# Reordering the first layer norm, one input load and two groups of short matmuls in a two-branch kernel on one core

## The chip, the cores and the metric

The kernel runs on one core of a Trainium2 chip. The metric is the device time of one execution in microseconds (us). All times inside the kernel are counted from the start of the profiled span.

## The reference, cut to what matters

```python
def reference(A_x, A_wqkv, A_w_phi, A_wo, B_x, B_w1, B_w2, B_w3, B_w4):
    xn = layernorm(A_x)                       # A_x is (1, 2048, 448); all bf16
    return A_x + A(xn, A_wqkv, A_w_phi, A_wo) + B(xn, B_w1, B_w2, B_w3, B_w4)

def A(x, wqkv, w_phi, wo):                    # linear attention, 16 heads of 28
    q, k, v = heads(x @ wqkv)
    phi(t) = concat(softmax(t @ w_phi), softmax(-t @ w_phi))
    kv, z  = phi(k).T @ v, sum(phi(k))        # sums over the 2048 rows
    return merge((phi(q) @ kv) / (phi(q) @ z + 1e-6)) @ wo

def B(x, w1, w2, w3, w4):                     # MLP with shifted columns
    h  = gelu(layernorm(x) @ w1)              # w1, w2: 448 x 448
    x1 = x + shift_quarters(h) @ w2
    return x1 + gelu(layernorm(x1) @ w3) @ w4 # w3: 448 x 1792, w4: 1792 x 448
```

The layer norm is over the 448 columns of one row. B normalises its input again; the kernel uses the once normalised rows for the product with w1.

## The kernel before

**Tiles.** The 2048 rows are 16 tiles of 128 rows (tile 0 to 15) and 4 groups of 4 tiles. `xtok` holds x, `xn` the normalised rows, `xnT` their transposes, with the 448 columns on partitions in four chunks of 128 (kc 0 to 3). 448 is not a multiple of 128: the chunks start at columns 0, 128, 192 and 320, and chunks 1 and 2 overlap by 64 columns. So a product over the 448 columns is three matmuls over 128 rows ("fulls") and one over 64 rows ("tail").

**Quads.** `quad` (L454) computes four such products into four PSUM banks: first the twelve fulls, three for each bank, with small jobs ("fills") put behind each bank's three; then the four tails. A tail uses rows 0 to 63 for an even bank and rows 64 to 127 for an odd one, so two of them run at a time in the two halves of the array. `w1_quad(g, ...)` (L470) does group g's product with w1 (output 112 x 512 for each bank) and empties the banks, two at a time, with a GELU on ScalarE into `hT`. `v_quad(i, ...)` (L477) does V of tiles i to i+3 (128 x 448 each) and empties the banks with copies into `vaug`, on ScalarE for the first eight tiles.

**The first layer norm** (L417 to L425, called at L626 to L634). For each tile VectorE makes the statistics (`ln_stats`: bn_stats and bn_aggr), GpSimd turns the variance into a scale (`ln_scale`: an add and a power of -1/2, into `rs`), and VectorE, or GpSimd for tiles 8, 10, 12 and 14, applies mean and scale (`ln1_apply`, written `xn<-xtok`). The program order on VectorE is written out: for tiles 0 to 7, statistics of tile i and then the normalise of tile i-1. From tile 8 on it goes by pairs.

**Loads** (L337 to L351). x tiles 0 to 3 come one by one, from the queues of SyncE (SP) and ScalarE; `load_x(4, 4)`, `load_x(8, 4)` and `load_x(12, 4)` bring four tiles in one transfer of 448 KB each, from SyncE. The V columns of wqkv (`wv`) and `w1` come in two halves of 224 KB each; w1 from ScalarE's queue. Behind the x loads SyncE issues w2, wphi and eight transposing loads of Wqkv (`wT`, in the region `hi`).

**Order of work on TensorE** (L635 to L648). After some matmuls that only keep it busy (`spin`), TensorE transposes tiles 0 to 11 itself: `xn_T(i, b)` (L445) is four transposes into bank b and one copy by ScalarE into `xnT`. The transposes of tiles 2 and 3 are fills of the V quad of tile 0, those of 4 to 7 fills of the W1 quad of group 0, and so on:

```python
v_quad(0, (4, 5, 6, 7), ([(xn_T, 2, 2)], [(xn_T, 3, 3)]))
w1_quad(0, (0, 1, 2, 3), ([], [], [(xn_T, 4, 4), (xn_T, 5, 5)], [(xn_T, 6, 6), (xn_T, 7, 7)]))
v_quad(4, (4, 5, 6, 7), ([], [], [(xn_T, 8, 0)], [(xn_T, 9, 1)]))
w1_quad(1, (0, 1, 2, 3), ([], [(xn_T, 10, 4)], [(xn_T, 11, 5)], [(phi_blocks,)]))
for i in range(12, 16):
    xn_Td(i)
```

Tiles 12 to 15 are transposed by DMA from SyncE's queue (`xn_Td`, L451), which then loads w3, wo and w4. The W1 quads of groups 2 and 3 follow, with `fold` (L438) as fills: it multiplies wphi into the Q and K columns of Wqkv, through banks 0 and 1 in group 2's quad and banks 4 and 5 in group 3's. `phi_blocks` (L431) makes the block matrix `bd` for it, with a product on VectorE. Then come the K and Q quads, the w2 products, the attention and the MLP (L658 on), about 160 us that the change doesn't touch.

**Waits.** A recorder (L18 to L185) keeps the order of each engine as it is written, finds for each instruction what it must wait for, and emits the waits. An engine's instructions run in program order, so one that waits holds all behind it on that engine. Every operation has the line of a recorder's helper in the profile: L188 is a matmul, L192 a transpose on TensorE, L196 a ScalarE activation, L200 an operation of VectorE or GpSimd, L203 a transposing DMA, L206 a plain DMA.

Of the kernel before, what the change touches and what calls it, by code (L numbers as in the profile page):

```python
# [5 lines left out]
ACT = mybir.ActivationFunctionType  # L6
# [202 lines left out]
def bass_parallel_sum__linear_kernel_hedgehog__mixer_s_mlp__prompt_kernel(  # L209
    nc, A_x, A_wqkv, A_w_phi, A_wo, B_x, B_w1, B_w2, B_w3, B_w4, out,  # L210
):
    _, S, D = A_x.shape
    H, DH = A_w_phi.shape[0], A_w_phi.shape[1]
    F = B_w3.shape[1]
    assert (S, D, H, DH, F) == (2048, 448, 16, 28, 1792)
    NT, NG, KC, NC, NM, FC, HP = 16, 4, 4, 4, 4, 14, 32
    CR = 112
# [5 lines left out]
    with es:  # L223
        R = Recorder(nc, es)
# [9 lines left out]
        def view(h, cols, dt=BF16, at=0):  # L234
            a = h[:, at // 2:at // 2 + cols * DTB[dt] // 2]
            return a if dt == BF16 else a.bitcast(dt)

        def new(name, cols, dt=BF16):
            return view(region(name, cols * DTB[dt]), cols, dt)

        pairs = []
        for b in range(4):
            t = es.enter_context(nc.psum_tensor("bank%d%d" % (2 * b, 2 * b + 1), [128, 1024], F32))
            R.track(t, 4096, psum=True)
            pairs.append(t)
        banks = [pairs[b // 2][:, 512 * (b % 2):512 * (b % 2) + 512] for b in range(8)]
# [5 lines left out]
        xnT = view(xnT_r, KC * S).rearrange("p (c s) -> p c s", c=KC)  # L252
        hT_r = region("hT", NM * HW * 2)
        hT = view(hT_r, NM * HW).rearrange("p (m s) -> p m s", m=NM)
# [3 lines left out]
        vaug = view(vaug_r, NT * 512).rearrange("p (t c) -> p t c", t=NT)  # L258
        gT = new("gT", 2 * KC * 512).rearrange("p (b c s) -> p b c s", b=2, c=KC)
# [4 lines left out]
        wv = new("wv", KC * D).rearrange("p (c d) -> p c d", c=KC)  # L264
# [4 lines left out]
        w1 = view(w1_r, KC * D).rearrange("p (c d) -> p c d", c=KC)  # L269
        w2 = new("w2", NM * D).rearrange("p (m d) -> p m d", m=NM)  # L270
        wo = new("wo", KC * D).rearrange("p (c d) -> p c d", c=KC)
        w3 = new("w3", KC * F).rearrange("p (c f) -> p c f", c=KC)
# [50 lines left out]
        dve, pool = "DVE", "POOL"  # L323


        def load_x(i, n, eng="SP"):
            R.dma(xtok[:, i:i + n, :], x2d[128 * i:128 * (i + n), :].rearrange("(j p) d -> p j d", p=128), eng)
# [5 lines left out]
        def load_lap(dst, src, engs=("SP", "SP")):  # L333
            for h in range(2):
                R.dma(dst[:, 2 * h:2 * h + 2, :], src[192 * h:192 * h + 256, :].rearrange("(c p) d -> p c d", p=128), engs[h])
# [3 lines left out]
        load_x(2, 1)  # L339
        load_lap(wv, A_wqkv[:, 896:1344], ("ACT", "SP"))  # L340
        load_x(3, 1, "ACT")
        load_x(4, 4)
        load_lap(w1, B_w1, ("ACT", "ACT"))
        load_x(8, 4)
        load_x(12, 4)
# [53 lines left out]
        def halves(a):  # L399
            return a.rearrange("p (b e) -> p b e", b=2)  # L400
# [12 lines left out]
        def ln_apply(eng, dst, src, mvt, rst, i):  # L413
            m, op = (mvt[:, i, 0:1], ALU.subtract) if eng == dve else (rst[:, i, 1:2], ALU.add)
            R.ew(eng, "tensor_scalar", dst, src, m, rst[:, i, 0:1], op0=op, op1=ALU.mult)
# [6 lines left out]
        def ln1_apply(eng, i):  # L422
            ln_apply(eng, halves(xn[:, i, :]), lap(xtok[:, i, :]), mv, rs, i)
# [27 lines left out]
        def xn_Td(i):  # L451
            R.dma_t(xnT[:, :, 128 * i:128 * i + 128], xn[:, i, :])

        def quad(outs, lhs, rhs, fills=(), more=()):  # L454
            for k in range(4):
                for kc in (0, 3, 2 - k % 2):
                    R.mm(outs(k), lhs(k, kc, 0, 128), rhs(k, kc, 0, 128), kc == 0, False)
                if k < len(fills):
                    for f in fills[k]:
                        f[0](*f[1:])  # L460
            for k in range(4):
                kc, lo = 1 + k % 2, 64 * (k % 2)
                R.mm(outs(k), lhs(k, kc, lo, lo + 64), rhs(k, kc, lo, lo + 64), False, True)
            for f in more:
                f()

        def two(b):
            return pairs[b // 2].rearrange("p (b e) -> p b e", b=2)

        def w1_quad(g, bs, fills=()):  # L470
            quad(lambda k: banks[bs[k]][0:CR, :],
                 lambda m, kc, lo, hi: w1[lo:hi, kc, CR * m:CR * m + CR],
                 lambda m, kc, lo, hi: xnT[lo:hi, kc, 512 * g:512 * g + 512], fills)
            for m in (0, 2):
                R.act(hT[0:CR, m:m + 2, 2 + 512 * g:2 + 512 * g + 512], two(bs[m])[0:CR, :, :], ACT.Gelu_apprx_tanh)

        def v_quad(i, bs, fills=()):  # L477
            quad(lambda k: banks[bs[k]][:, 0:D],
                 lambda k, kc, lo, hi: xnT[lo:hi, kc, 128 * (i + k):128 * (i + k) + 128],
                 lambda k, kc, lo, hi: wv[lo:hi, kc, :], fills)  # L480
            for k in (0, 2):
                vd = vaug[:, i + k:i + k + 2, :].rearrange("p t (h e) -> p t h e", e=HP)[:, :, :, 0:DH]
                vs = two(bs[k])[:, :, 0:D].rearrange("p t (h e) -> p t h e", e=DH)
                if i < 8:
                    R.act(vd, vs, ACT.Copy)
                else:
                    R.ew(dve, "tensor_copy", vd, vs)

        def kq_quad(i, bs):
            g, c = divmod(i, 4)  # L490

            def outs(k):
                return banks[bs[k]][:, 0:D] if k < 2 else banks[bs[k]][0:CR, :]

            def lhs(k, kc, lo, hi):
                if k < 2:
                    return xnT[lo:hi, kc, 128 * (i + k):128 * (i + k) + 128]
                return wpq[lo:hi, kc, CR * (c + k - 2):CR * (c + k - 1)]

            def rhs(k, kc, lo, hi):  # L500
                return wpk[lo:hi, kc, :] if k < 2 else xnT[lo:hi, kc, 512 * g:512 * g + 512]

            quad(outs, lhs, rhs)
            for s in range(2):
                R.act(phik[:, i:i + 2, s, :], two(bs[0])[:, :, 0:D], ACT.Exp, scale=1.0 - 2.0 * s)
            e = (eq_lo if g < 2 else eq_hi)[0:CR, c:c + 2, :, 512 * (g % 2):512 * (g % 2) + 512]
            for s in range(2):
                R.act(e[:, :, s, :], two(bs[2])[0:CR, :, :], ACT.Exp, scale=1.0 - 2.0 * s)
# [79 lines left out]

        def w3_quad(q, more=()):
            gf = [divmod(4 * q + k, FC) for k in range(4)]  # L590
            quad(lambda k: banks[k][:, :],
                 lambda k, kc, lo, hi: w3[lo:hi, kc, 128 * gf[k][1]:128 * gf[k][1] + 128],
                 lambda k, kc, lo, hi: gT[lo:hi, gf[k][0] % 2, kc, :], (), more)
            for k in (0, 2):
                g, fc = gf[k]
                R.act(h3T[:, g % 2, fc:fc + 2, :], two(k), ACT.Gelu_apprx_tanh)
# [28 lines left out]

        for i in range(8):  # L626
            ln1_stats(i, 1, 0)
            if i > 0:
                ln1_apply(dve, i - 1)
        for i in range(8, NT, 2):  # L630
            ln1_stats(i, 2, 1)
            ln1_apply(pool, i)
            ln1_apply(dve, i - 1)
# [2 lines left out]
        xn_T(0, 0)  # L636
        spin(5, 128)
        xn_T(1, 1)
        v_quad(0, (4, 5, 6, 7), ([(xn_T, 2, 2)], [(xn_T, 3, 3)]))
        w1_quad(0, (0, 1, 2, 3), ([], [], [(xn_T, 4, 4), (xn_T, 5, 5)], [(xn_T, 6, 6), (xn_T, 7, 7)]))  # L640
        v_quad(4, (4, 5, 6, 7), ([], [], [(xn_T, 8, 0)], [(xn_T, 9, 1)]))
        w1_quad(1, (0, 1, 2, 3), ([], [(xn_T, 10, 4)], [(xn_T, 11, 5)], [(phi_blocks,)]))
        for i in range(12, 16):
            xn_Td(i)
        load_rest()
        late_3()
        w1_quad(2, (4, 5, 6, 7), [[(fold, 1, m, m % 2)] for m in range(NM)])
        w1_quad(3, (0, 1, 2, 3), [[(fold, 0, m, 4 + m % 2)] for m in range(NM)])  # L648
        ring = [0]

        def take(n):
            r = [2 * ((ring[0] + k + 2) % 3) for k in range(n // 2)]
            ring[0] += n // 2
            return [b + j for b in r for j in (0, 1)]
# [3 lines left out]
        for ps in range(8):  # L658
            kq_quad(2 * ps, take(4))
            if ps in kvs:  # L660
                kv_tile(kvs[ps][0])
            late = [(kv_tile, i) for i in kvs.get(ps, (0, 0) if ps else (0,))[1:]]
            if ps in w2s:
                b = take(2)
                for i in w2s[ps]:
                    w2_tile(i, b[i % 2], False)
                    for f in late[0:1]:
                        f[0](*f[1:])
                    late = late[1:]
                k_norm(2 * ps)  # L670
                for i in w2s[ps]:
                    ln_stats(st2, mv2, xn, i)
                    if i % 4 == 3:
                        ln_scale(mv2, rs2, i - 3, 4, 4)
            else:
                v_quad(8 if ps == 1 else 12, take(4), (late,))
                k_norm(2 * ps)
                g_apply(ps - 1)
                g_apply(ps)
            if ps in (2, 4):  # L680
                g_T(ps - 2)
                g_T(ps - 1)
# [76 lines left out]
```

The softmax here doesn't subtract the row's maximum and nothing guards it: scores larger than these inputs give would overflow.

## Time and profile before

| | us |
|---|---|
| median of 4 runs | 196.65 (196.51 to 196.99) |
| the profiled execution | 196.1 |
| its span, first to last instruction | 194.4 |
| TensorE (PE) busy | 185.6 (95%) |
| VectorE (DVE) busy | 110.5 (57%) |
| GpSimd (POOL) busy | 98.1 (50%) |
| ScalarE (ACT) busy | 81.0 (42%) |

How to read the lines that follow. A timeline row has the start, the duration, the engine, the line of the code, the operation, what is written and what is read, the count of instructions merged, and in brackets the idle time of the engine just before, with what ended it. A row of the chain of work (the chain that ended last, followed back from the last instruction) has the start, the duration, and the engine with what it wrote. A row of DMA issues has the queue, the count, KB and the median us from issue to landing. PE is a matmul, PEld a weight load; SPq is SyncE's DMA queue. TensorE's granted clock is full from 6.9 us on.

### The profile page before, as it was taken

The numbers are of one execution on the slowest core, as the hardware profiler recorded it, in microseconds if no ns is written. First come the engines' busy times: TensorE is split into PE (matmuls) and PEld (weight loads), VectorE is DVE, ScalarE is ACT, GpSimd is POOL, SyncE is SP. The second block draws the span as 40 slices with busy tenths as digits, with TensorE's granted clock in tenths as the row PEclk, the third lists the DMA queues.
The fourth block names the chain that finished last, engine by engine and source line by source line (L and its number), as shares of the span: only waits on it lengthen the run. The fifth ranks groups of instructions, "written<-read, shape, count | busy, mean of one in ns | idle before, by whom it ended". The sixth has DMA issues, their size and how long they took to land.

```text
span 194.4 us, 2922 instructions
## 1 busy us (share of the span) xinstructions
PE 185.6 (95%) x1125; PEld 93.8 (48%) x1135; DVE 110.5 (57%) x264; ACT 81.0 (42%) x95; POOL 98.1 (50%) x151
## 2 busy tenths in 40 slices
PE   7699999999999999999899999999999999999994
PEld 4455555444455545544445445444454445464451
DVE  4799600499959999965256437163173616656031
ACT  2349788943775666834550330123120330303000
POOL 5568840054974996893624424841434034276140
PEclk9999999999999999999999999999999999999999
DMA  5994359900020100004002441402253021222211
GB/s 172 367 195 83 76 107 403 343 20 0 0 54 3 35 19 0 3 16 92 0 15 42 81 82 28 77 0 74 54 84 78 24 51 30 51 51 61 67 47 47
DMA packets 32956, 14.74 MB, mean 76 GB/s; under 512 B 24687, under 2 KB 32431, under 8 KB 32943
## 3 DMA queue, kind: packets, MB, share of 16 engines
q1 hardware_dynamic: 31694, 13.58, 28.6%
q10 hardware_dynamic: 1248, 0.98, 1.6%
q8 instruction: 9, 0.15, 0.3%
q14 instruction: 5, 0.03, 0.1%
HBM read 7.08 MB, written 1.84 MB: 46 GB/s over the span
## 4 chain that ended last, share of the span: by engine, by line
PE 85%; ACT 4%; DVE 3%; DMA 3%; issue 1%; POOL 1%; SPq 1%; DVEq 0%
PE bank L188 84%; DMA xtok<-in_A_x_dram 3%; ACT phik L196 2%; DVE vaug L200 2%; PE bank L192 1%; ACT eq_lo L196 1%; POOL phik L200 1%; SPq L206 1%; DVE ksum L200 1%; DVE xn L200 1%; ACT hT L196 0%; DVE st L200 0%; ACT xnT L196 0%; ACT wpk L196 0%; DVE rks L200 0%
## 5 line engine op out<-in xcount | busy, mean ns | idle before, releaser
L196 ACT ACTIVATE phik<-bank 128x1024 bf16<-128x1024 f32 (+1 forms) x44 | 40.9, 982 | 86.9 <-PE bank L188 86.8
L200 DVE TENSOR_TENSOR vaug<-bank,vaug 128x464 f32<-128x464 f32 (+3 forms) x65 | 32.7, 513 | 31.3 <-PE bank L188 29.7
L188 PE MATMUL bank<-gT,w 128*128 128x512 bf16 (+1 forms) x214 | 44.8, 380 | 1.2 <-ACT phik L196 0.7
L188 PE MATMUL bank<-w,phik 128*128 128x448 bf16 x224 | 45.1, 353 | 0.8 <-DVE vaug L200 0.8
L200 POOL TENSOR_TENSOR xnT<-vaug 128x196 bf16<-128x196 f32 (+1 forms) x32 | 18.1, 587 | 49.4 <-DVE vaug L200 49.4
L200 POOL TENSOR_TENSOR phik<-phik,rks 128x896 bf16<-128x896 bf16 x16 | 26.8, 1699 | 22.8 <-DVE rks L200 22.8
L188 PEld LDWEIGHTS bank<-w,phik 128*128 128x128 bf16 x224 | 21.0, 98 | 20.2 <-DVE vaug L200 1.7
L188 PEld LDWEIGHTS bank<-gT,w 128*128 128x128 bf16 (+1 forms) x224 | 17.7, 97 | 24.7 <-issue 5.9
L200 POOL TENSOR_TENSOR vaug<-xn,xtok 128x448 f32<-128x448 bf16 x16 | 16.4, 1033 | 5.1 <-DVE vaug L200 5.1
L200 DVE TENSOR_TENSOR xn<-bank,xn 128x256 bf16<-128x256 f32 (+1 forms) x32 | 10.7, 378 | 13.6 <-PE bank L188 13.3
L200 DVE RECIPROCAL vaug<-bank 128x16 f32<-128x16 f32 x16 | 4.1, 254 | 22.7 <-PE bank L188 22.7
L200 DVE TENSOR_REDUCE ksum<-phik 128x32 f32<-128x896 bf16 x16 | 16.8, 1052 | 0.0
L188 PE MATMUL bank<-xnT,wpq 128*112 128x512 bf16 (+1 forms) x64 | 14.9, 381 | 0.3 <-ACT eq_lo L196 0.3
L188 PE MATMUL bank<-xnT,w 128*112 128x512 bf16 (+1 forms) x64 | 15.1, 386 | 0.0
L188 PE MATMUL bank<-wo,xnT 128*128 128x448 bf16 (+1 forms) x64 | 14.5, 352 | 0.0
L188 PE MATMUL bank<-w,hT 112*128 112x448 bf16 x64 | 14.3, 353 | 0.0
L188 PE MATMUL bank<-wpk,xnT 128*128 128x448 bf16 (+1 forms) x64 | 13.3, 355 | 0.0
L188 PE MATMUL bank<-wv,xnT 128*128 128x448 bf16 (+1 forms) x64 | 12.8, 354 | 0.1
L200 POOL TENSOR_SCALAR g_tok<-xn,rs 128x512 bf16<-128x512 bf16 x16 | 12.1, 774 | 0.0
L200 POOL TENSOR_TENSOR rs<-mv,mhalf 128x1 f32<-128x1 f32 (+2 forms) x16 | 11.3, 706 | 1.3
L200 DVE BATCH_NORM_STATS2 st<-xtok 128x6 f32<-128x448 bf16 x16 | 9.8, 611 | 1.9 <-DMA xtok<-in_A_x_dram 1.9
L200 DVE BATCH_NORM_STATS2 st<-xn 128x6 f32<-128x448 bf16 x16 | 9.4, 589 | 0.1
(62 smaller groups left out, 177.8 us busy)
## 6 DMA issues: line engine op xcount, KB each, us to landing
w<-in_B_w_dram SPq DMA_DIRECT2D x2, 896.0 KB, 5.8
out_dram<-vaug SPq DMA_DIRECT2D x15, 112.0 KB, 1.9
w<-in_B_w_dram SPq DMA_DIRECT2D x1, 1568.0 KB, 11.9
xtok<-in_A_x_dram SPq DMA_DIRECT2D x3, 448.0 KB, 7.6
w<-in_B_w_dram ACTq DMA_DIRECT2D x2, 224.0 KB, 6.3
wo<-in_A_wo_dram SPq DMA_DIRECT2D x2, 224.0 KB, 6.8
w<-in_B_w_dram SPq DMA_DIRECT2D x1, 392.0 KB, 9.1
gT<-g_tok SPq DMA_TRANSPOSE x16, 2.5
```

Source lines behind the costliest of these rows:

```text
L188: self.op("PE", lambda e: e.matmul(out, lhsT, rhs, start=start, stop=stop, skip_group_check=True), [out], [lhsT, rhs])
L192: self.op("PE", lambda e: e.transpose(out, in_, ident), [out], [in_, ident])
L196: self.op("ACT", lambda e: e.activation(out, in_, func, **kw), [out], [in_] + aps)
L200: self.op(eng, lambda e: getattr(e, name)(out, *args, **kw), [out], aps)
L206: self.op(eng, lambda e: e.dma_start(out, in_), [out], [in_], dma=True)
```

## The change

Tile 3's normalise is put ahead of tile 4's statistics on VectorE. The load of tiles 4 to 7 becomes two transfers of two tiles. `quad` is taken apart into `fulls` and `tails`, which take a flag that tells whether they come first for their banks. A new function `octet` runs the V quad of tile 0 and the W1 quad of group 0 as one: V's fulls, V's tails, W1's tails (now the first of their sums), the copies that empty V's banks, W1's fulls with their fills, and the GELUs. All other quads run as before, through `alone`.

```diff
-        load_x(4, 4)
+        load_x(4, 2)
+        load_x(6, 2)
         load_lap(w1, B_w1, ("ACT", "ACT"))
...
+        def fulls(p, first, fills=()):
+            outs, lhs, rhs = p
             for k in range(4):
                 for kc in (0, 3, 2 - k % 2):
-                    R.mm(outs(k), lhs(k, kc, 0, 128), rhs(k, kc, 0, 128), kc == 0, False)
+                    R.mm(outs(k), lhs(k, kc, 0, 128), rhs(k, kc, 0, 128), first and kc == 0, not first and kc == 2 - k % 2)
                 if k < len(fills):
                     for f in fills[k]:
                         f[0](*f[1:])
+
+        def tails(p, first):
+            outs, lhs, rhs = p
             for k in range(4):
                 kc, lo = 1 + k % 2, 64 * (k % 2)
-                R.mm(outs(k), lhs(k, kc, lo, lo + 64), rhs(k, kc, lo, lo + 64), False, True)
+                R.mm(outs(k), lhs(k, kc, lo, lo + 64), rhs(k, kc, lo, lo + 64), first, not first)
...
+        def octet(p, p_fills, p_out, q, q_fills, q_out):
+            fulls(p, True, p_fills)
+            tails(p, False)
+            tails(q, True)
+            p_out()
+            fulls(q, False, q_fills)
+            q_out()
...
         for i in range(8):
             ln1_stats(i, 1, 0)
-            if i > 0:
+            if i not in (0, 4):
                 ln1_apply(dve, i - 1)
+            if i == 3:
+                ln1_apply(dve, 3)
...
-        v_quad(0, (4, 5, 6, 7), ([(xn_T, 2, 2)], [(xn_T, 3, 3)]))
-        w1_quad(0, (0, 1, 2, 3), ([], [], [(xn_T, 4, 4), (xn_T, 5, 5)], [(xn_T, 6, 6), (xn_T, 7, 7)]))
-        v_quad(4, (4, 5, 6, 7), ([], [], [(xn_T, 8, 0)], [(xn_T, 9, 1)]))
-        w1_quad(1, (0, 1, 2, 3), ([], [(xn_T, 10, 4)], [(xn_T, 11, 5)], [(phi_blocks,)]))
+        v, w = v_parts(0, (4, 5, 6, 7)), w1_parts(0, (0, 1, 2, 3))
+        octet(v[0], ([(xn_T, 2, 2)], [(xn_T, 3, 3)]), v[1],
+              w[0], ([], [], [(xn_T, 4, 4), (xn_T, 5, 5)], [(xn_T, 6, 6), (xn_T, 7, 7)]), w[1])
+        alone(v_parts(4, (4, 5, 6, 7)), ([], [], [(xn_T, 8, 0)], [(xn_T, 9, 1)]))
+        alone(w1_parts(1, (0, 1, 2, 3)), ([], [(xn_T, 10, 4)], [(xn_T, 11, 5)], [(phi_blocks,)]))
```

`v_parts` and `w1_parts` return the operands of the former `v_quad` and `w1_quad` and the function that empties the banks.

More of the change, by code (lines that the diff above doesn't have):

```diff
@@ L452, in xn_Td @@
             R.dma_t(xnT[:, :, 128 * i:128 * i + 128], xn[:, i, :])
-        def quad(outs, lhs, rhs, fills=(), more=()):
+        def fulls(p, first, fills=()):
+            outs, lhs, rhs = p
             for k in range(4):
                 for kc in (0, 3, 2 - k % 2):
-                    R.mm(outs(k), lhs(k, kc, 0, 128), rhs(k, kc, 0, 128), kc == 0, False)
+                    R.mm(outs(k), lhs(k, kc, 0, 128), rhs(k, kc, 0, 128), first and kc == 0, not first and kc == 2 - k % 2)
                 if k < len(fills):
@@ L460, in quad @@
                         f[0](*f[1:])
+        def tails(p, first):
+            outs, lhs, rhs = p
             for k in range(4):
                 kc, lo = 1 + k % 2, 64 * (k % 2)
-                R.mm(outs(k), lhs(k, kc, lo, lo + 64), rhs(k, kc, lo, lo + 64), False, True)
+                R.mm(outs(k), lhs(k, kc, lo, lo + 64), rhs(k, kc, lo, lo + 64), first, not first)
+        def quad(p, fills=(), more=()):
+            fulls(p, True, fills)
+            tails(p, False)
             for f in more:
@@ L465, in quad @@
                 f()
+        def octet(p, p_fills, p_out, q, q_fills, q_out):
+            fulls(p, True, p_fills)
+            tails(p, False)
+            tails(q, True)
+            p_out()
+            fulls(q, False, q_fills)
+            q_out()
         def two(b):
             return pairs[b // 2].rearrange("p (b e) -> p b e", b=2)
[L470 to L487, printed above, removed]
+        def w1_parts(g, bs):
+            def evac():
+                for m in (0, 2):
+                    R.act(hT[0:CR, m:m + 2, 2 + 512 * g:2 + 512 * g + 512], two(bs[m])[0:CR, :, :], ACT.Gelu_apprx_tanh)
+            return (lambda k: banks[bs[k]][0:CR, :],
+                    lambda m, kc, lo, hi: w1[lo:hi, kc, CR * m:CR * m + CR],
+                    lambda m, kc, lo, hi: xnT[lo:hi, kc, 512 * g:512 * g + 512]), evac
@@ new lines, in v_parts, with evac @@
+        def v_parts(i, bs):
+            def evac():
+                for k in (0, 2):
+                    vd = vaug[:, i + k:i + k + 2, :].rearrange("p t (h e) -> p t h e", e=HP)[:, :, :, 0:DH]
+                    vs = two(bs[k])[:, :, 0:D].rearrange("p t (h e) -> p t h e", e=DH)
+                    if i < 8:
+                        R.act(vd, vs, ACT.Copy)
+                    else:
+                        R.ew(dve, "tensor_copy", vd, vs)
+            return (lambda k: banks[bs[k]][:, 0:D],
+                    lambda k, kc, lo, hi: xnT[lo:hi, kc, 128 * (i + k):128 * (i + k) + 128],
+                    lambda k, kc, lo, hi: wv[lo:hi, kc, :]), evac
@@ L489, in kq_quad, with alone @@
+        def alone(parts, fills=()):
+            quad(parts[0], fills)
+            parts[1]()
         def kq_quad(i, bs):
@@ L501, in rhs @@
                 return wpk[lo:hi, kc, :] if k < 2 else xnT[lo:hi, kc, 512 * g:512 * g + 512]
-            quad(outs, lhs, rhs)
+            quad((outs, lhs, rhs))
             for s in range(2):
@@ L590, in w3_quad @@
             gf = [divmod(4 * q + k, FC) for k in range(4)]
-            quad(lambda k: banks[k][:, :],
-                 lambda k, kc, lo, hi: w3[lo:hi, kc, 128 * gf[k][1]:128 * gf[k][1] + 128],
-                 lambda k, kc, lo, hi: gT[lo:hi, gf[k][0] % 2, kc, :], (), more)
+            quad((lambda k: banks[k][:, :],
+                  lambda k, kc, lo, hi: w3[lo:hi, kc, 128 * gf[k][1]:128 * gf[k][1] + 128],
+                  lambda k, kc, lo, hi: gT[lo:hi, gf[k][0] % 2, kc, :]), (), more)
             for k in (0, 2):
@@ L646, in bass_parallel_sum__linear_kernel_hedgehog__mixer_s_mlp__prompt_kernel @@
         late_3()
-        w1_quad(2, (4, 5, 6, 7), [[(fold, 1, m, m % 2)] for m in range(NM)])
-        w1_quad(3, (0, 1, 2, 3), [[(fold, 0, m, 4 + m % 2)] for m in range(NM)])
+        alone(w1_parts(2, (4, 5, 6, 7)), [[(fold, 1, m, m % 2)] for m in range(NM)])
+        alone(w1_parts(3, (0, 1, 2, 3)), [[(fold, 0, m, 4 + m % 2)] for m in range(NM)])
         ring = [0]
@@ L675, in bass_parallel_sum__linear_kernel_hedgehog__mixer_s_mlp__prompt_kernel @@
             else:
-                v_quad(8 if ps == 1 else 12, take(4), (late,))
+                alone(v_parts(8 if ps == 1 else 12, take(4)), (late,))
                 k_norm(2 * ps)
```

## The prediction

> **What bounds the kernel now.** I read the page's first part and its chain of work, then that chain in order of time over the first 35 us (the change touches nothing that is issued later), then the timeline of the stretches on it, and last the queue of SyncE.
>
> ```profile
> PE 185.6 (95%) x1125; PEld 93.8 (48%) x1135; DVE 110.5 (57%) x264; ACT 81.0 (42%) x95; POOL 98.1 (50%) x151
> PE 85%; ACT 4%; DVE 3%; DMA 3%; issue 1%; POOL 1%; SPq 1%; DVEq 0%
> ```
>
> TensorE is the bound: busy for 95% of the span and 85% of the chain. A change pays only where TensorE stands still, and only if it doesn't stand still again further on. The chain in order of time (start, us, what) shows where it does:
>
> ```profile
> 2.20 6.41 DMA xtok<-in_A_x_dram
> 8.63 0.64 DVE st L200
> 9.48 0.31 DVE xn L200
> 9.83 0.41 PE bank L192 x4
> ...
> 27.59 0.54 ACT wpk L196
> 28.14 0.93 ACT hT L196
> 29.06 0.05 issue
> 29.11 6.02 PE bank L188 x41
> ```
>
> Up to 9.83 the chain is the load of x tiles 4 to 7, VectorE's statistics of tile 4 (8.63), and only then tile 3's normalise (9.39, ends 9.77), for which TensorE's transposes of tile 3 wait. At 29.11 it is a GELU (ACT hT) that must empty bank 4. What tile 3 itself needs is there much earlier (timeline, VectorE, GpSimd and TensorE rows):
>
> ```profile
> 7.62 0.55 POOL L200 TENSOR_TENSOR rs<-mv,mhalf 128x1 f32<-128x1 f32 x1
> 8.63 0.63 DVE L200 BATCH_NORM_STATS2 st<-xtok 128x6 f32<-128x448 bf16 x1 [1.14 <-DMA xtok<-in_A_x_dram]
> 9.39 0.38 DVE L200 TENSOR_SCALAR xn<-xtok,mv,rs 128x512 bf16<-128x512 bf16 x1
> 9.83 0.40 PE L192 MATMUL bank<-ident,xn 128*128 128x128 bf16 x4 [1.32 <-DVE xn L200]
> ```
>
> Its scale is ready at 7.62 + 0.55 = 8.17. VectorE is held at 8.63 by a load that tile 3 doesn't need, and TensorE idles 1.32 us.
>
> **Part 1, tile 3 first.** Tile 2's normalise began 0.04 after its scale (7.04, then 7.08) and took 0.41. So tile 3's begins at 8.21 and ends at 8.62; 0.05 later (as 9.77, then 9.83) its transposes begin, at 8.67 instead of 9.83: **-1.16 us** at this point of TensorE. No instruction is added.
>
> What is queued behind it on VectorE: tile 4's statistics. They start 0.33 after a normalise that waited for its scale (10.49, then 10.82), so at 8.54 instead of 8.63. All later tiles hang on them. From tile 4 on GpSimd is the bound of the normalising: its add and pow take 1.13 us a tile without a gap to spare (adds at 10.61, 11.74, 12.88), and the pairs from tile 8 on 2.2 us (17.02, 19.24, 21.45). Removing tile 3's normalise from between the statistics of tiles 4 and 5 gives these nothing, since GpSimd can't take tile 5 before it is done with tile 4. So **everything from tile 4's normalise to tile 15's comes only 0.09 earlier**, while TensorE comes 1.16 earlier. This decides the forecast.
>
> **Part 2, the split load.** One more issue on SyncE, 0.47 long (the 448 KB issue at 2.20), ahead of x8, x12, w2, wphi and the eight transposes of Wqkv. The landing of a 224 KB half beside its twin isn't in the trace. Bounds: wv's 224 KB, issued just ahead on the same queue, took 4.5 (2.20 + 4.5 = 6.7); w1's 224 KB on the other queue at most 6.7 (8.9). I take 8.5 or earlier, since it is the first half of a transfer that lands at 8.61 now. Below 8.54 it is worth nothing more, as tile 3's normalise is ahead; at 8.9 tile 4 would be 0.27 later than now instead of 0.09 earlier, and the gain smaller by 0.36. Without the split tile 4 would start at 8.63 again, so the split is worth 0.09. Tiles 6 and 7 are needed at 10.73 (statistics 10.82 now); their last bytes are last of the same 448 KB, at 8.6 plus one issue, about 9.1, and even the whole transfer behind landed at 2.71 + 7.6 = 10.3. That one (tile 8, needed at 13.0) and x12 (3.26 + 8.8 = 12.1, needed at 17) have room for 0.5 us.
>
> [...]
>
> **Part 3, the tails side by side.** The switch between 128-row and 64-row matmuls shows as a gap. The last V full streams until 11.49, the tails start at 11.59 (0.10); their second pair ends at 11.98, the W1 fulls start at 12.07 (0.09); the first 512-column matmul after a switch is followed after 0.26 instead of 0.214 (0.05). W1's own tails have the same two gaps (15.60 to 15.69, 16.17 to 16.26). With W1's tails behind V's, two switches go: 0.10 + 0.09 + 0.05 + 0.01 = **0.25 us**. Tails of 128 and of 112 columns do follow each other without a gap (35.06, 35.26, next at 35.57); were that otherwise here, the 0.25 is lost. The W1 tails now need w1 at 10.8: its halves landed by 2.74 + 6.7 = 9.5.
>
> [...]
>
> **The sum along TensorE.** Start times after, with those of before in brackets:
>
> - V's last three fulls 9.76 (10.92), V tails 10.43 (11.59), W1 tails 10.83, W1 fulls 10.83 + 0.22 + 0.21 + 0.10 = 11.36 (12.07).
> - Transposes of tile 4: 11.36 + 1.99 = 13.35 (14.06); last W1 fulls 13.79; tile 6: 14.44 (15.15); tile 7 could go at 14.66, but its normalise ends at 14.94 - 0.09 = 14.85: it goes at 14.90. A first new wait, 0.24.
> - V quad of tile 4: 15.12 (16.26), so -1.14. Transposes of tile 8, 1.71 on: 16.83; they need bank 0, emptied by W1's first GELU. ScalarE's four copies start 0.42 after tile 4's transposes (13.77) and take 2.07 before that GELU: 15.84 + 0.97 = 16.81. So 16.87 (17.98): -1.11.
> - From there nothing waits: tile 9's normalise ends at 17.0 (wanted 17.66), 10's at 19.07 (19.8), 11's at 19.22 (20.7); VectorE's product for bd comes at 23.3 (fold wants it at 23.5). The last W1 quad would start at 28.07 - 1.1 = 26.97.
>
> **But it needs tiles 12 to 15, and these are transposed by DMA:**
>
> ```profile
> 20.60 0.77 POOL L200 TENSOR_SCALAR xn<-xtok,rs 128x512 bf16<-128x512 bf16 x1
> 21.39 5.16 SPq L203 DMA_TRANSPOSE xnT<-xn  x4
> xnT<-xn SPq DMA_TRANSPOSE x4, 2.5
> ```
>
> The four go out back to back from 21.39, when GpSimd has tile 12 (20.60 + 0.77 = 21.37); the last starts at 25.29 and lands 2.5 later, at 27.83. That is 0.24 ahead of need now. After, tile 12 is ready at 21.28, the last lands at 27.74, and TensorE waits for it from 26.97 to about 27.76 (0.02 from landing to start, as at 8.61 and 8.63): **a new wait of 0.79 us, which takes the place of the one removed**. It hides the 0.25 of part 3 entirely, the waits for tile 7 and for bank 0 too. Then one old wait goes: the three fulls last 0.68 (28.07 to 28.75), and before, the fold had to wait until 29.11 for bank 4's GELU. That GELU now ends at about 27.97. The fold starts at 27.76 + 0.68 = 28.44 instead of 29.11: **-0.67 us**. Behind it all is paced by TensorE or follows it (the VectorE and GpSimd steps of the chain at 39 to 43 wait for its matmuls), so the rest moves as a block.
>
> The profiled execution: 196.1 (span 194.4 and 1.7 around it), so 195.43. It lies 0.55 under the median, 196.65; against the median, **195.98**.
>
> **The rivals.**
>
> 1. The whole gain arrives: 1.1 us, 195.55. For it: 1.32 us of idle is really removed. Against: tile 15 would have to land at 26.97, so tile 4's statistics would have to start 0.86 earlier than now, and tile 3's scale (8.17) is ahead of them. It needs GpSimd's loop to be quicker than its rows. 8%.
> 2. The split lands tile 4 late (8.9) or the wait on the transposes costs some tenths more: the gain is 0.3, 196.35. For it: w1's 224 KB took up to 6.7. Against: wv's took 4.5. 15%.
> 3. Slower: SyncE comes late to tile 12. The eight transposes of Wqkv end at 20.01, and tile 12 waits until 21.39, which leaves 1.38. One issue more takes 0.47. But two of the eight took 2.79 and 2.24 to issue instead of 1.26. If two more take 2.5, SyncE is free at 20.01 + 0.47 + 2.5 = 22.98, tile 15 lands at 29.4, the fold starts at 30.15: +1.0, 197.7. It costs from 21.28 on, and makes the kernel slower once SyncE is free later than 21.95. Against: those long issues fall where x still loads, and waiting there is not added twice. 9%.
> 4. The octet doesn't save its switches, or costs as much: 0.25 to 0.5 on TensorE at 10.8. It falls into the wait of 0.79 and changes nothing: part of the forecast.
>
> **How the numbers follow.** The forecast has 68%, with its own range of 195.7 to 196.3 (tile 4's start known to 0.1, the median's scatter of 0.2). The range 195.5 to 196.5 takes in rivals 1 and 2. About 0.2%, 0.39 us, is what a measurement of this kernel can tell from no change: faster by more, 0.65 of the 0.68, rival 1 and a little of rival 2, 0.76; within, 0.15; slower, 0.09.
>
> **What the new profile would show.** Right: tile 3's transposes at 8.67 without the idle time of 1.32; tile 4's statistics at 8.54, tile 12's normalise ending near 21.28; a TensorE wait of about 0.8 before the last W1 quad, at 27.7; the fold behind it near 28.4, with no wait for the GELU; the same lag of 0.67 to the end. Wrong: tile 4's statistics waiting for a DMA after 8.6; the DMA transposes of tile 12 starting after 21.4; that W1 quad starting near 27.0.

## The result and the profile after

The changed kernel takes 195.97 us (median), before 196.50 beside it: ratio 0.9978, 95% interval 0.9969 to 0.9986, or 0.43 us faster (0.28 to 0.61). The forecast was 195.98, that is 0.67 faster than the 196.65 shown first. That the median falls on it is luck: before itself came out 0.15 lower over its 78 executions than over the first four, and the measured gain is two thirds of the forecast one, whose 0.67 lies above the interval. The two profiled executions hide even this gain: 196.1 before, which is early for that kernel, and 196.15 after, both with a span of 194.4. Why is a part of the answer.

The first part of the page and the chain by engine, after:

```profile
PE 184.9 (95%) x1125; PEld 93.2 (48%) x1135; DVE 110.3 (57%) x264; ACT 81.1 (42%) x95; POOL 97.5 (50%) x151
PE 77%; DVE 6%; POOL 5%; DMA 4%; ACT 3%; issue 2%; SPq 1%; ACTq 0%; DVEq 0%
```

TensorE's share of the chain fell from 85% to 77%; VectorE, GpSimd and the DMA took it over. The chain in order of time shows where (start, us, what):

```profile
1.75 5.10 DMA xtok<-in_A_x_dram
6.87 0.64 DVE st L200
...
8.73 0.41 DVE xn L200
9.14 0.55 DVE st L200
...
20.84 0.77 POOL xn L200
...
25.77 2.52 DMA xnT<-xn
28.29 0.14 issue
28.42 8.81 PE bank L188 x56
```

It no longer runs along TensorE from 9.8 on. It goes from tile 3's load (landed 6.84) through tile 3's normalise (8.73), tile 4's statistics, GpSimd's loop and the DMA transposes of tiles 12 to 15 to 28.42. VectorE's, TensorE's and SyncE's rows of the timeline:

```profile
9.06 0.62 DVE L200 BATCH_NORM_STATS2 st<-xtok 128x6 f32<-128x448 bf16 x1
9.20 0.40 PE L192 MATMUL bank<-ident,xn 128*128 128x128 bf16 x4 [0.17 <-DVE xn L200]
11.35 2.67 PE L188 MATMUL bank<-xnT,w 64*112 64x512 bf16 x13
13.86 0.61 PE L192 MATMUL bank<-ident,xn 128*128 128x128 bf16 x8
15.50 1.87 PE L188 MATMUL bank<-wv,xnT 128*128 128x448 bf16 x9
28.42 0.83 PE L188 MATMUL bank<-xnT,w 128*112 128x512 bf16 x3 [0.76 <-DMA xnT<-xn]
29.08 0.36 PE L188 MATMUL bank<-bd,hi 112*128 112x112 bf16 x4
```

```profile
21.63 5.40 SPq L203 DMA_TRANSPOSE xnT<-xn  x4
```

The idle 1.32 us before tile 3's transposes is 0.17; W1's tails and fulls are one block of 13. The forecast's new wait is there, 0.76 us at 28.42, and the fold at 29.08 no longer waits for the GELU. In this pair of profiles the fold is only 0.03 earlier than before (29.08 and 29.11), where 0.67 was forecast.

### The profile page after: what moved, and what is told of

Read it like the earlier page. It is cut to its first block, busy times and chain, and to the rows that moved or that the text cites. A ratio compares the mean times of both kernels' runs of the same rounds, so it can differ in the third digit from the quotient of the medians.

```text
span 194.4 us, 2923 instructions
## 1 busy us (share of the span) xinstructions
PE 184.9 (95%) x1125; PEld 93.2 (48%) x1135; DVE 110.3 (57%) x264; ACT 81.1 (42%) x95; POOL 97.5 (50%) x151
## 4 chain that ended last, share of the span: by engine, by line
PE 77%; DVE 6%; POOL 5%; DMA 4%; ACT 3%; issue 2%; SPq 1%; ACTq 0%; DVEq 0%
PE bank L188 77%; DMA xtok<-in_A_x_dram 3%; POOL rs L200 2%; ACT phik L196 2%; DVE vaug L200 2%; DVE st L200 2%; DVE xn L200 1%; DMA xnT<-xn 1%; POOL xn L200 1%; SPq L203 1%; ACT eq_lo L196 1%; POOL phik L200 1%; POOL mv L200 1%; DVE mv L200 1%; DVE ksum L200 1%
```

## The experiments

Theory: the gain that TensorE has by the first V quad is held at the last W1 quad by the DMA transposes of tiles 12 to 15, which hang on tile 4's statistics through GpSimd. Rivals: the split load does the harm; the parts each bring their own share; the gain is lost elsewhere. Ratios are against before, timed beside each kernel. e1 to e4, e5 to e8 and e9 to e12 were timed as three groups on three chips, so ratios of different groups can't be told apart by a tenth or two of a per cent.

| kernel | median us | ratio (95% interval) |
|---|---|---|
| the change | 195.97 | 0.9978 (0.9969 to 0.9986) |
| e1: one load for tiles 4 to 7 | 195.68 | 0.9971 (0.9950 to 0.9993) |
| e2, e11: octet only | 196.90, 196.81 | 1.0028 (0.9999 to 1.0058), 1.0026 (1.0002 to 1.0050) |
| e3: no octet | 195.90 | 0.9978 (0.9960 to 0.9996) |
| e4, e5: transposes free | 195.56, 195.62 | 0.9965 (0.9937 to 0.9992), 0.9944 (0.9918 to 0.9971) |
| e6: tile 3 first only | 196.35 | 0.9982 (0.9961 to 1.0003) |
| e7: tile 12 on TensorE | 195.86 | 0.9943 (0.9921 to 0.9964) |
| e8: e7, one load, folds later | 195.51 | 0.9933 (0.9908 to 0.9958) |
| e9: tile 3's load first | 195.71 | 0.9958 (0.9932 to 0.9983) |
| e10: the same in the kernel before | 197.34 | 1.0047 (1.0015 to 1.0079) |
| e12: e8 with tile 3's load first | 196.01 | 0.9960 (0.9929 to 0.9990) |

**e1, the whole load.** Edit of the changed kernel:

```diff
-        load_x(4, 2)
-        load_x(6, 2)
+        load_x(4, 4)
```

> The changed kernel with tiles 4 to 7 in one transfer again; the rest of the change stays. Theory (the end is set by the DMA transposes of tiles 12 to 15, which hang on tile 4's statistics): these start when the whole transfer lands, near 8.6, instead of after tile 3's normalise; up to 0.1 us slower than the changed kernel, so 0.3 to 0.45 faster than before; TensorE still waits 0.7 to 0.8 for the transposes. Rival (the split itself makes tile 3's load land late, 6.84 in the profile of the changed kernel against 5.64 before, and with it the whole normalising): tile 3's load lands below 6.3 again and the kernel is 0.2 to 0.5 us faster than the changed one.

0.9971, not separable from the change; its interval doesn't exclude the rival's 0.2 us. In its profile the load landed at 8.3 and tile 4's statistics started at 8.52, behind tile 3's normalise, and TensorE still idles 0.82 before the last W1 quad (27.96). Tile 3's load landed at 5.9; but e2, e6 and e8 have one load too and there tile 3's statistics started as late as 7.16 to 7.62. So the loads don't support the rival: tile 3's load scatters with either form.

**e2 and e11, the octet alone** (the order on VectorE and the load as before):

> Only the octet; the order on VectorE and the load are those of before. Theory: TensorE is 0.25 us earlier from 16.2 on, the DMA transposes come as before, at 27.8, just when the last W1 quad is ready for them, so nearly all of it arrives: 0.2 us faster than before. Rival (the octet's saving is not real, or it is covered by other waits): 0.0.

> The octet alone once more: its first measurement said 0.0 to 1.1 us slower, against a theory of 0.2 faster, and its profile showed TensorE at half clock from 10.9 to 14.3 after tiles 4 to 7 landed at 9.6. Theory (that is the scatter of the executions, not the octet): between 0.2 slower and 0.4 faster than before, and in a profile at full clock V quad 4 starts about 0.25 earlier after tile 3's transposes than before (6.43 after them in the profile before, 6.2 here). Rival (the octet alone costs): slower again by 0.3 or more.

Both say 0.3% slower, so the 0.2 us of gain that was expected is refuted. (Two of e2's twelve executions and one of e11's hold a stretch at half clock, by their mean clock of 0.991 (see the last section); without these their means are still 0.3 us above those of before.) TensorE's rows in e11:

```profile
10.22 0.40 PE L192 MATMUL bank<-ident,xn 128*128 128x128 bf16 x4 [1.39 <-DVE xn L200]
16.42 1.86 PE L188 MATMUL bank<-wv,xnT 128*128 128x448 bf16 x9
18.54 0.38 PE L192 MATMUL bank<-ident,xn 128*128 128x128 bf16 x4 [0.26 <-ACT hT L196]
29.39 0.39 PE L188 MATMUL bank<-xnT,w 128*112 128x512 bf16 x1 [0.70 <-DMA xnT<-xn]
```

The switches are saved: V quad 4 starts 6.20 after tile 3's transposes (16.42 - 10.22), before 6.43 (16.26 - 9.83). But the transposes of tile 8 come 8.32 after them, before 8.15 (17.98 - 9.83). W1's tails now stand ahead of tile 4's transposes, so ScalarE's four copies and the GELU behind them come later, and tile 8's transposes wait for the GELU's bank. 0.23 is saved and 0.40 given back within two quads. That this makes the whole kernel 0.5 us slower isn't shown: the end in this profile is again the wait on the DMA transposes (0.70), of which the first took 2.16 us to issue instead of 1.22. What stretched it stays open.

**e3, no octet** (the first two quads one after the other):

> The changed kernel without the octet: the first V quad and the first W1 quad run one after the other, each with its own tails. Theory: TensorE loses the 0.25 of the switches and, more, has nothing to do while it waits for tile 7's normalise (the W1 tails stood there), 0.6 us at 16; but its wait for the DMA transposes shrinks by the same, so the end moves by at most 0.2: 0.25 to 0.45 faster than before. Rival (what TensorE gains early arrives at the end): 0.4 to 0.6 us slower than the changed kernel, so about as slow as before.

0.9978, the same ratio as the change's: no worth of the octet is seen at the end, though the interval would hide 0.2%.

```profile
15.05 0.40 PE L192 MATMUL bank<-ident,xn 128*128 128x128 bf16 x4 [0.38 <-DVE xn L200]
28.17 0.83 PE L188 MATMUL bank<-xnT,w 128*112 128x512 bf16 x3 [0.36 <-DMA xnT<-xn]
```

TensorE waits 0.38 for tile 7's normalise, and 0.40 less than after the change (0.36 instead of 0.76) for the transposes. What is lost early is only waited less later: the mechanism shows in the rows, not in the times.

**e4 and e5, transposes that depend on nothing late.** The rows of tiles 12 to 15 get other data:

```diff
-            R.dma_t(xnT[:, :, 128 * i:128 * i + 128], xn[:, i, :])
+            R.dma_t(xnT[:, :, 128 * i:128 * i + 128], xn[:, i - 12, :])
```

> The changed kernel, but the four DMA transposes for tiles 12 to 15 read the normalised tiles 0 to 3, which are ready early; so these four tiles' transposed rows hold other data, and the output is not the reference's. The same number of transposes of the same size in the same place of the queue. Theory: they no longer hang on the normalising, start when the queue is free (20.5 to 21) and land before TensorE wants them; the wait of 0.76 goes, and the kernel is 0.3 to 0.5 us faster than the changed one, about 0.8 to 1.1 faster than before. Rival (the transposes come late because the queue is late, or TensorE loses the time elsewhere): less than 0.15 faster than the changed kernel.

> The changed kernel with the DMA transposes for tiles 12 to 15 reading tiles 0 to 3 (the output is not the reference's in the rows of these tiles); the same edit as before, since that run's profile shows TensorE some five times slower throughout and can't be read. Theory (the wait on the transposes is what keeps TensorE's gain from the end): no TensorE wait for a DMA before the last W1 quad, the wait of the fold for the GELU is back (0.2 to 0.4), and the kernel is 0.35 to 0.5 us faster than the changed one. Rival (lost elsewhere): within 0.15 of the changed one.

0.9965 and 0.9944, faster than the change's 0.9978, but both intervals reach its own; the times alone don't show it. e5's rows:

```profile
9.28 0.40 PE L192 MATMUL bank<-ident,xn 128*128 128x128 bf16 x4 [0.17 <-DVE xn L200]
27.11 1.54 PE L188 MATMUL bank<-xnT,w 64*112 64x512 bf16 x7
28.73 0.37 PE L188 MATMUL bank<-bd,hi 112*128 112x112 bf16 x4
```

The last W1 quad's fulls stand in one block with the tails ahead of them (x7), without a marked wait for a DMA. The fold comes 19.45 after tile 3's transposes, in the changed kernel 19.88 (29.08 - 9.20): 0.43 that the transposes held. The rest of the 0.76 is the GELU, which the fold waits for again (it ends at 28.68). The fulls may still have waited some 0.14 for the transposes: SyncE was free only at 20.80, the last of them landed at about 27.6, and the fulls start 0.71 after the tails, where 0.57 is enough in e7. So SyncE's own queue is the next limit, close behind. That the transposes of late tiles held TensorE is the forecast's mechanism, and these rows show it.

**e6, tile 3 first and nothing else:**

> Only tile 3's normalise ahead of tile 4's statistics; one load for tiles 4 to 7, no octet. Theory: the octet's saving and the split's lie before the wait on the transposes and are worth nothing at the end, so this edit alone gives what the whole change gives, 0.3 to 0.5 us faster than before, with a smaller wait on the transposes (0.2 to 0.5 instead of 0.76). Rival (each part brings its own share): at most 0.25 faster than before.

0.9982: most of the change's gain, as the theory has it, but the interval takes in both no change and the whole gain. Its profile can't be set beside the others: TensorE ran at half clock from 8.4 to 11.8 in it (read in the windows below).

**e7 and e8, taking the wait away with the right data.** e7 transposes tile 12 on TensorE; e8 has one load, and moves the folds behind the second three fulls, through four banks:

```diff
-        ... [(phi_blocks,)]))
-        for i in range(12, 16):
+        ... [(phi_blocks,), (xn_T, 12, 6)]))
+        for i in range(13, 16):
...
-        alone(w1_parts(3, (0, 1, 2, 3)), [[(fold, 0, m, 4 + m % 2)] for m in range(NM)])
+        alone(w1_parts(3, (0, 1, 2, 3)), [[], [(fold, 0, 0, 4)], [(fold, 0, 1, 5), (fold, 0, 2, 6)], [(fold, 0, 3, 7)]])
```

> The changed kernel, but tile 12 is transposed by TensorE, behind phi_blocks, through bank 6, and only tiles 13 to 15 by DMA. TensorE gets 0.22 us more work; three DMA transposes from tile 13's normalise (21.5 to 21.8) on land one issue, 1.3 us, earlier, at 26.6 to 27.0. Theory: the wait before the last W1 quad is gone or under 0.1, the fold waits for the GELU again, and the kernel is 0.1 to 0.3 us faster than the changed one. Rival (the wait isn't what holds the gain): 0.0 to 0.25 slower than the changed one.

> As the last one, with one load for tiles 4 to 7, and the folds of the last two W1 quads one place later, through four banks instead of two, so that none of them waits for a GELU. Theory: the two waits for the GELU at the start of these quads (0.3 and 0.36 in the profile before) go too, and TensorE runs without a stop from the transposes of tile 8 to the K and Q quads: 0.7 to 1.0 us faster than the changed kernel, 1.2 to 1.4 faster than before. Rival (the next limit, the three DMA transposes or ScalarE's copies, takes most of it): 0.3 to 0.5 faster than the changed one.

e7: no wait for the DMA, and the fold waits for the GELU again; 0.9943, its interval below the changed kernel's, though the median is only 0.1 under it.

```profile
28.78 0.37 PE L188 MATMUL bank<-bd,hi 112*128 112x112 bf16 x4 [0.20 <-ACT hT L196]
```

e8 moves the folds of group 2 in the same way. 0.9933, the fastest here, its interval too below the changed kernel's: 0.45% or about 0.9 us by the ratios, 0.46 by the medians. Its chain from the transposes of tile 8 (18.76) on is TensorE alone; the last of it, up to 35 us:

```profile
23.91 0.33 PE bank L192 x4
24.24 10.86 PE bank L188 x78
```

This profile is of an execution that took 196.51, though, 1.0 above the median: TensorE's matmuls were slow in it until about 10.5.

```profile
7.13 1.33 PE L188 MATMUL bank<-wv,xnT 128*128 128x448 bf16 x3
9.23 1.33 PE L188 MATMUL bank<-wv,xnT 128*128 128x448 bf16 x3
18.98 0.73 PE L188 MATMUL bank<-wv,xnT 128*128 128x448 bf16 x3
```

In the profile of before, three such matmuls took 0.78 at 6.82 and 0.73 at 7.78, and four transposes 0.61 at 6.42 and 0.40 at 7.55. That change of pace is what "full from 6.9 us on", said of before, rests on; the granted clock itself is 1.00 over the whole span of before, ahead of 6.9 too, and 1.00 from 0.3 to 13.95 in this profile. What slowed the matmuls isn't shown. In e12, the same kernel with one load moved, TensorE is more than 1 us earlier (tile 12's transposes at 22.58 instead of 23.84), and the wait for the DMA transposes, of tiles 13 to 15 now, is back:

```profile
27.95 1.47 PE L188 MATMUL bank<-xnT,w 128*112 128x512 bf16 x6 [0.30 <-DMA xnT<-xn]
```

So the TensorE without a stop is shown only for an execution in which TensorE is late; the profile of e12 shows that the transposes can hold it again where it is not.

**e9, e10 and e12, tile 3's load first** on ScalarE's queue:

```diff
+        load_x(3, 1, "ACT")
         load_lap(wv, A_wqkv[:, 896:1344], ("ACT", "SP"))
-        load_x(3, 1, "ACT")
```

> The changed kernel with tile 3's load ahead of wv's first half on ScalarE's queue; nothing else moves. In the changed kernel's profiles seen so far tile 3's statistics wait for this load (start 6.6 to 7.0, against 6.28 before), and the statistics of all later tiles are behind them. Theory (after the change the end hangs on tile 3's load, through tile 3's scale, tile 4's statistics, GpSimd's loop and the DMA transposes): tile 3's statistics start at 6.2 to 6.4 and the kernel is 0.2 to 0.5 us faster than the changed one, 0.6 to 1.0 faster than before. Rival (wv lands later instead and TensorE waits for it, or the transposes come late for another reason): within 0.15 of the changed kernel.

> The kernel before with the same swap of two loads. Theory: there the statistics of tile 4 wait for the load of tiles 4 to 7, far behind tile 3's, so an earlier tile 3 is worth nothing: within 0.2 us of before. Rival (the early loads matter by themselves, whatever the order on VectorE): 0.3 or more faster.

> Everything that helped together: tile 3's normalise first, the octet, one load for tiles 4 to 7, tile 12 transposed by TensorE, the folds one place later through four banks, and tile 3's load ahead of wv's. Theory: 0.2 to 0.5 faster than the same without the swapped loads, 1.5 to 2.0 us faster than before. Rival (TensorE's early waits, now for wv, bring it to half clock): no faster than without the swap.

e9: tile 3's statistics start at 6.61 without waiting for a load (all starts are 0.34 later there because tile 0 landed later), the wait on the transposes is 0.50, and the ratio 0.9958 against 0.9978: in the expected direction, with overlapping intervals. e10 went the other way, 0.9 us slower than before, and refutes "within 0.2": the wait of TensorE for wv (0.96) is not on the chain of its profile, which goes through the load of tiles 4 to 7 (landed 10.15) to tile 3's transposes at 11.38, behind a wait of 1.79. The granted clocks show a second cost. Five of e10's twelve executions have a mean clock of 0.983 to 0.991 over the span; the stretch at half clock in the profiles of e2 and e6 leaves 0.991 (last section). With e9 and e12, which take tile 3's load first too, it is 10 of 34; of before beside them it is 3 of 33, of the changed kernel 1 of 54. So such executions were more frequent with the swap, as the rival named for e12 would have it; that early waits bring the half clock isn't shown. They aren't all of e10's loss: without those five its mean is 197.19, before's beside it 196.55. e12 gained nothing over e8. VectorE's row for tile 4 in e12:

```profile
9.18 0.63 DVE L200 BATCH_NORM_STATS2 st<-xtok 128x6 f32<-128x448 bf16 x1 [0.36 <-DMA xtok<-in_A_x_dram]
```

With tile 3 early, the unsplit load of tiles 4 to 7 is what VectorE waits for. e8 with the split and the swap wasn't tried.

## Why the prediction was right, step by step

- **Tile 3 first:** right in direction, not in size. The idle 1.32 went; -1.16 was forecast and -0.63 came (9.83 to 9.20 in the profiles), with the transposes at 9.20 instead of 8.67, since tile 3's load landed at 6.84 and its statistics waited (6.87; 6.28 before). The forecast took that load from one execution. Other profiles of both forms have 6.3 to 7.6.
- **"Everything behind tile 4's statistics comes only 0.09 earlier", and the DMA transposes then hold TensorE:** the mechanism is right (0.76 of wait, 0.79 forecast; e5 takes most of it away). That the wait itself agrees is luck in part, since both of its ends moved: TensorE was ready 0.69 later than forecast (27.66, not 26.97) and the last landing came 0.55 later, 0.25 of it by a slower issue, the rest, like TensorE's, behind tile 3's late load. The size of the gain was off: tile 4's statistics started at 9.06 (8.54 forecast), tile 12 was ready at 21.60 (21.28), the first DMA transpose took 1.47 to issue (1.22), so the last landed at 28.29 (27.74). From landing to TensorE's start it took 0.13, where 0.02 was taken from a load and VectorE. The sum, 0.32 + 0.25 + 0.11 = 0.68, is what the fold is later than forecast (29.08 instead of 28.44), within 0.04. The start of the transposes at 21.63 is one of the prediction's own signs of being wrong (after 21.4); it came since tile 12 was late, not since SyncE was. "1.13 us a tile without a gap to spare" misread the rows. The loop runs through VectorE's statistics as well as GpSimd, and GpSimd waited in it already before, and waits in it after:

```profile
11.74 0.34 POOL L200 TENSOR_SCALAR mv<-mv 128x1 f32<-128x1 f32 x1 [0.16 <-DVE mv L200]
12.09 0.26 POOL L200 TENSOR_SCALAR mv<-mv 128x1 f32<-128x1 f32 x1 [0.38 <-DVE mv L200]
```

(The first row is of before, the second of after.) After, the adds came 0.91, 1.20 and 1.05 apart, and from the start of tile 4's statistics to the end of tile 12's normalise it took 12.54, before 12.74: 0.2 was won.
- **The split is worth 0.09:** the term rests on a landing at 8.61. Where tiles 4 to 7 come in one transfer, tile 4's statistics waited for it until 9.02 (e11), 9.18 (e12), 9.61 (e2) and 10.17 (e10); in the five readable profiles with two transfers they started at 8.73 to 9.14 and never waited for it. In flight the whole load took 6.1 to 8.0 us (eight profiles), the first half of the split one 5.5 to 6.2 (five). So the profile of before was an early execution (196.1 against a median of 196.5), and where the whole load is late, the split may be worth more than 0.09. Not everywhere: in e1, e6 and e8, with one load, tile 4's statistics (8.52, 9.35, 9.82) didn't wait for it. The second halves landed 6.0 to 7.0 us after their issue, at 8.7 to 9.7: near the 9.1 of the sum. A timed pair that differs by the split alone (e3 and e6, 0.9978 and 0.9982; the change and e1) doesn't separate it.
- **The octet:** as said. The 0.25 of switches is real (6.43 to 6.20 in e11) and hidden. The delay of ScalarE's copies behind the earlier W1 tails was in the sum: tile 4's transposes come 4.66 after tile 3's (4.68 forecast, 4.23 before). The sum had the 0.25 given back in two waits, 0.24 for tile 7 and 0.04 for bank 0's GELU. In the changed kernel it is 0.10 in place of the first (the eight transposes at 14.95 take 0.71, not 0.61) and 0.16 ahead of tile 8's transposes; in e11, with tile 3 late and so no wait for tile 7, all 0.26 is the GELU's. (For the 0.16 the profile names GpSimd, but tile 8's normalise ends at 17.20 and the GELU at 17.37, and the transposes start at 17.52. The GELU is the likelier cause, which isn't shown.) The 0.2 of gain that was expected of the octet alone didn't follow from this sum.
- **The old GELU wait goes:** right; the fold starts 0.66 after the quad (0.68), and with the DMA wait gone the GELU wait returns (e5, e7).
- **Rival 2 (gain 0.3):** the 0.43 lies nearer to it than to the 0.67. Its first condition, a half that lands at 8.9, didn't come (the first halves landed at 7.7 to 8.4); its second, that the transposes cost some tenths more, did.
- **Rival 3 (SyncE late):** didn't happen. SyncE was free at 20.86 instead of 20.01, 0.74 ahead of tile 12 (21.60). Only the first issue behind it was slower, by 0.25.

## What to carry to other kernels

Before costing a wait that is removed, follow what the waiting engine needs last, further on, and which engine makes it: TensorE gained 0.6 us at 9 us in the profiles (1.16 forecast), and the loop of VectorE and GpSimd, which gained little, took most of it back at 28 us through a DMA. An edit whose gain lies ahead of such a wait is worth nothing behind it, as long as the wait is longer than the gain. Where a chain begins with a load, one profile gives one landing: take its scatter from several before an 0.1 us term is built on it.

## What the runs showed of the hardware

**A stretch at half clock in some executions.** In the profile of e6 TensorE's granted clock is 0.50 from 8.38 to 11.79, in that of e2 from 10.91 to 14.32, 3.41 us both times, and 1.00 in the stretches of that length before and behind. The three stretches (columns: stretch, length, PE, PEld, DVE, ACT and POOL busy, PEclk, DMA share, GB/s) in e6:

```profile
4.96:8.38 3.42, 1.77 (x18) 0.97 (x18) 2.54 (x7) 1.19 (x2) 1.99 (x6) 1.00 1.06 357
8.38:11.79 3.41, 3.41 (x15) 1.82 (x16) 2.48 (x7) 1.19 (x2) 1.82 (x5) 0.50 1.14 303
11.79:15.20 3.41, 3.41 (x25) 1.85 (x24) 3.27 (x11) 1.76 (x3) 1.91 (x5) 1.00 1.39 147
```

and in e2:

```profile
7.49:10.91 3.42, 1.22 (x10) 0.54 (x10) 2.26 (x7) 0.82 (x2) 1.09 (x4) 1.00 1.08 368
10.91:14.32 3.41, 3.41 (x16) 1.36 (x17) 3.31 (x10) 0.78 (x2) 2.68 (x7) 0.50 1.51 127
14.32:17.73 3.41, 3.41 (x26) 2.04 (x23) 3.27 (x10) 2.04 (x4) 2.25 (x5) 1.00 0.67 129
```

In the 3.42 us before, TensorE was busy 1.77 (e6) and 1.22 (e2), its longest wait 0.71 and 1.27. Waits alone don't tell when the half clock comes: in the profile of e10 TensorE stood idle for 0.96 and 1.79 us between 7.1 and 11.4, and its mean clock over the span is 1.000. What brings it, no run tells. The executions of e2 with a mean clock of 0.991 took 198.61 and 198.59 us, its other ten 195.70 to 197.57; that of e6 took 197.01, its other eleven 195.93 to 196.75. The profile of e2 has a late load as well (tiles 4 to 7 landed at 9.6, and TensorE waited 1.27 until 10.81 for tile 3's normalise behind it).

**The first DMA transpose of a group** took 1.22 (before), 1.23 (e9), 1.47 (after), 2.05 (e6) and 2.16 us (e11) to issue, the three behind it 1.26 to 1.27 in before and after, on the same queue and for the same size; no run tells what sets it.
